# The first four units of a gated linear attention with a bilinear feed-forward behind it, laid out anew

## Chip, cores and metric

One core of a Trainium2 chip. The metric is device time in microseconds (us) of one execution. The engines are TensorE (PE, matmul; PEld is its weight load), VectorE (DVE), ScalarE (ACT), GpSimd (POOL) and SyncE (SP, which issues most DMAs). Each works through its own instructions in program order and waits only where one of them needs something that another engine or a DMA has not delivered yet.

## What is computed

```python
f = 1.0 / (1.0 + np.exp(-f_logit))                 # B, H, S, D = 4, 8, 768, 48
for t in range(S):
    state = f[:, :, t, :, None] * state + np.einsum('bhd,bhe->bhde', k[:, :, t], v[:, :, t])
    y[:, :, t] = np.einsum('bhd,bhde->bhe', q[:, :, t], state)
x = y.transpose(0, 2, 1, 3).reshape(B * S, H * D)  # 3072 x 384
out = (x @ w_a) * (x @ w_b) @ w_out                # d_ff 1536; weights arrive as float64
```

## The kernel before

**Units.** The attention is cut into 16 units: one batch, half of the sequence (384 tokens) and four heads each. Units 0 and 1 make block 0 of x (384 tokens x 384 channels), units 2 and 3 the second half of the same batch, block 1, and so on. There are three sets of input tiles (q, k, f, v); unit u uses set u % 3. Units 0 to 3 are written out by hand; the later ones and the feed-forward are laid by a planner with costs and due times, which the change doesn't touch.

**A unit's front** (`front_parts`, four parts): ACT takes two sigmoids of f (L301, L304), POOL an affine (L307); DVE scans the running products of f forward (`scan_f`, L311, and a small check L314); DVE restarts and scans the inverse in six pieces (L319, L324); DVE multiplies q by the products and k by the inverses (`times`, L328).

**A unit's core**: `scores` (PE, q against k, L374), `mask` (DVE, L397), `turn` (PE transposes of k, L409) and `turned` (ACT copies them to kT, L411), `gains` (PE, kT against v, L433), `carry` (DVE adds them up to states, L454, L456) and `hand_on` (DVE, L465, for the second half of the sequence), `within` (PE, masked scores against v, L476), `across` (PE, states against q, L497), `out_of_bank` (copies of y out of PSUM, L522, on ACT, for units 0 and 1 partly on DVE) and `stored` (DMAs of y into xT, the transposed x of a block, L545).

**Feed-forward.** `up(blk, ft)` multiplies one 128-column tile of w_b and one of w_a by xT (three contraction tiles each, `emit`, L589), `product` copies the first to SBUF (ACT, L609) and multiplies (DVE, L611). Up to unit 3, five pairs of block 0 are spread over the hand-written order; then comes (1, 0), (1, 1), (0, 5) and so on.

**Weights.** Twenty pieces are loaded as 64-bit words (L249) and converted: `begin` does two steps of ACT work (L58, L59, then L62, L63) with a minimum on POOL (L60), `end` the last on DVE (L68, L70). Pieces 0 and 1 hold tile 0 of w_b and w_a, pieces 2 and 3 tiles 1 and 2, pieces 4 and 5 tiles 3 and 4, pieces 6 and 7 tiles 5 and 6. Pieces 4 and 5 are loaded into a part of `groups` that is free by then, the others into four places in turn.

**PSUM.** ps_x and ps_y have two banks each, ps_f0 to ps_f3 one each; `idle` lists those of ps_f that are free. Before, `scores` and `turn` took banks of ps_f when called with `spare`, else ps_x; gains always go to ps_x; y of unit 1 to ps_f, of the others to ps_y. The SBUF copy of y, `y_sb`, comes from a pool with one buffer, so unit 1's copies wait until unit 0's y is stored.

**Order.** A call in the hand-written part puts its instructions at the end of each engine's queue. So the order of the calls is the order on every engine, SP's too.

Of the kernel before, what the change touches and what calls it, by code (L numbers as in the profile page):

```python
# [26 lines left out]
R = 64  # L27
# [106 lines left out]
def by_quotients(ctx, tc, q, k, f_logit, v, moe_w_a, moe_w_b, moe_w_out, out, ident, weights, bad):  # L134
# [156 lines left out]
    def front_parts(u):  # L291

        t = sets[u % NSET]
        x = halves(t["f"])
        F = halves(products_of_f[u])
        inv = invs[u % 2 if u < 2 * NQ else 0]
        none = zero.broadcast_to((128, BLK))
        got = {}

        def sigmoid():  # L300
            nc.scalar.activation(F, x, AF.Sigmoid)  # L301

        def opposite():
            nc.scalar.activation(inv, x, AF.Sigmoid, bias=less, scale=-1.0, accum_out=tails[:, u:u + 1])  # L304

        def affine():
            nc.gpsimd.tensor_scalar(inv, inv, EXP_K, 1.0, ALU.mult, ALU.add)  # L307

        def scan_f(n):
            c = slice(n * BLK, n * BLK + BLK)  # L310
            nc.vector.tensor_tensor_scan(F[:, c], F[:, c], none, math.exp(MIDDLE), ALU.mult, ALU.add)  # L311

        def hold():
            nc.vector.tensor_tensor(held[:, u], products_of_f[u][:, :, BLK - 1], least, ALU.is_ge)  # L314

        def restart():
            got["start"] = sb2.tile([128, 2, NC - 1], FP32, tag="start", name="start")
            by_chunk = products_of_f[u].rearrange("p n (c m) -> p n c m", m=C)
            nc.vector.reciprocal(got["start"], by_chunk[:, :, 0:NC - 1, C - 1])  # L319

        def scan_inv(n, c):
            w = slice(n * BLK + c * C, n * BLK + c * C + C)
            first = got["start"][:, n, c - 1:c] if c else math.exp(-MIDDLE)
            nc.vector.tensor_tensor_scan(inv[:, w], inv[:, w], none[:, 0:C], first, ALU.mult, ALU.add)  # L324

        def times(nm, by):
            live.setdefault(u, {})
            nc.vector.tensor_tensor(halves(t[nm]), halves(t[nm]), by, ALU.mult)  # L328

        first = ((ACT, 930, opposite), (ACT, 750, sigmoid))  # L330
        return (
            [*(first[::-1] if u in FIRST else first), (POOL, 830, affine)],
            [(DVE, 870, scan_f, 0), (DVE, 870, scan_f, 1), (DVE, 80, hold)],
            [(DVE, 90, restart), *((DVE, 385, scan_inv, n, c) for n in range(2) for c in range(NC))],
            [(DVE, 880, times, "q", F), (DVE, 880, times, "k", inv)],
        )
# [9 lines left out]
    y_banks = [ps_y[:, p] for p in range(2)]  # L346
# [12 lines left out]
    def pair(spare=False):  # L359

        return [ps_f[idle.pop(0)] if spare else ps_x[:, i] for i in range(2)]

# [3 lines left out]
    def scores(u, spare=False):  # L366
        t = sets[u % NSET]
        qf, kf = halves(t["q"]), halves(t["k"])
        ps = pair(spare)
        for n, c, o in each():  # L370
            for h in range(2):
                for p in range(2):
                    r = slice(R * h, R * h + D)
                    nc.tensor.matmul(  # L374
                        ps[h][SUB * p:SUB * p + SUB, o:o + SUB],
                        lhsT=kf[r, tokens(n, c, p)],
                        rhs=qf[r, tokens(n, c, p)],
                        start=True,
                        stop=True,
                    )  # L380
        live[u]["scores"] = ps
        if spare is not None:
            mask(u, spare)

    def mask(u, spare=False):

        ps = live[u].pop("scores")
        at = sb1.tile([128, 2, BLK], FP32, tag="at", name="at")
        both = [(at[:, h], ps[h][:, 0:BLK]) for h in range(2)] if spare else [(at, ps_x[:, :, 0:BLK])]
        for to, x in both:  # L390
            lead = x.shape[1:-1]
            letters = "h"[:len(lead)]
            to, x = (y.rearrange(f"s {letters} (o t) -> s {letters} o t", t=SUB) for y in (to, x))
            tri = causal.unsqueeze(1)
            for _ in lead:
                tri = tri.unsqueeze(1)
            nc.vector.tensor_tensor(to, x, tri.broadcast_to((128, *lead, 2 * NC, SUB)), ALU.mult)  # L397
        live[u]["at"] = at
        give_back(ps)

    def turn(u, spare=False):

        kf = halves(sets[u % NSET]["k"])
        kT = sb1.tile([128, 2, NC, 128], FP32, tag="kT", name="kT")
        ps = pair(spare)
        for n in range(2):
# [3 lines left out]
            if spare:  # L410
                nc.scalar.copy(kT[:, n].rearrange("s c x -> s (c x)"), ps[n][:, 0:BLK])  # L411
        live[u]["kT"] = kT
        if not spare and spare is not None:
            turned(u)
        give_back(ps)

    def turned(u):

        nc.scalar.copy(live[u]["kT"].rearrange("s n c x -> s n (c x)"), ps_x[:, :, 0:BLK])

    def gains(u, all=True):
# [3 lines left out]
        last = half == NH - 1  # L425
        for n in range(2):
            for c in range(NC):
                for p in range(2):
                    if last and c == NC - 1 and p == 1:
                        continue  # L430
                    for h in range(2):
                        r = slice(SUB * p, SUB * p + SUB)
                        nc.tensor.matmul(  # L433
                            ps_x[R * h:R * h + D, p, (n * NC + c) * D:(n * NC + c) * D + D],
# [4 lines left out]
                        )  # L439
        st = sb3.tile([128, NJ, 2, D], FP32, tag="st", name="st")  # L440
        before = live[u - NQ]["st"][NJ] if half else None
        live[u]["st"] = [before] + [st[:, j] for j in range(NJ - 1 if last else NJ)]
        if all:
            for j in range(len(live[u]["st"]) - 1):
                carry(u, j)
            hand_on(u)

    def carry(u, j):
# [3 lines left out]
        new = ps_x[:, p, 0:2 * NC * D].rearrange("r (n c d) -> r n c d", n=2, c=NC)[:, :, c]  # L452
# [14 lines left out]
    def within(u, spare=False):  # L467

        t, at = sets[u % NSET], live[u]["at"]
        ps = live[u]["y"] = pair(True) if spare else y_banks  # L470
# [14 lines left out]
    def across(u, all=True):  # L485
# [4 lines left out]
        for n, c, o in reversed(list(each())) if half else each():  # L490
            for p in range(2):
# [13 lines left out]
        if all:  # L505
            for part in range(len(banks_of_y(u))):
                out_of_bank(u, part)
            stored(u)

    def banks_of_y(u):  # L510

        ps = live[u]["y"]
        whole = [(0, 0, 0, 128)] if ps[0] is y_banks[0] else [(0, 0, 0, D), (0, R, R, D)]
        return (*whole, (1, R, 0, D), (1, 0, R, D))

    def out_of_bank(u, part):

        if not part:
            live[u]["y_sb"] = sb1.tile([128, 2 * NC, 2, SUB], FP32, tag="y", name="y")
        p, e, r, rows = banks_of_y(u)[part]  # L520
# [10 lines left out]
    def stores_of(u):  # L531
# [4 lines left out]
        def begin():  # L536
            give_back(live[u].pop("y"))
# [4 lines left out]
        def store(n, h, kt, p, row, w):  # L542
            y = live[u]["y_sb"].rearrange("r (n c) p m -> r n (c p m)", n=2)
            queue = nc.scalar if u < NQ and (n + h) % 2 else nc.sync
# [323 lines left out]
    def core_parts(s):  # L868
# [3 lines left out]
        if u < 2 * NQ:  # L872
            yield PE, 1000, 0, scores, s, None
# [4 lines left out]
        if s < NU:  # L878
            yield DVE, 880, 0, mask, s
            yield PE, 850, 0, turn, s, None  # L880
            yield ACT, 700, 0, turned, s
        if u < 2 * NQ:
            yield PE, 1000, 0, gains, s, False
        elif s < NU:
            yield PE, 1550, 0, gains_and_across, u
        else:
            yield PE, 1000, 0, across, u, False
# [13 lines left out]
    def within_and_scores(u):  # L901
        within(u)
        scores(u + 1, None)

    def gains_and_across(u):
        gains(u + 1, False)
        across(u, False)
# [26 lines left out]
    with tc.manual_schedule():  # L934
# [9 lines left out]
        fronts = [front(u) for u in range(2 * NQ + 1)]  # L944


        load_unit(0, "f")
        load_unit(1, "f")
        next(fronts[0])
        load_unit(1, "q")  # L950
        load_unit(0, "q")
        load_unit(1, "k")
        load_weights()
        load_unit(0, "k")
        load_weights()
        patterns()
        next(fronts[0])
        load_weights()
        next(fronts[0])
        load_unit(1, "v")  # L960
        next(fronts[1])
        next(fronts[1])
        next(fronts[0])
        load_unit(0, "v")
        next(fronts[1])
        begin(3)
        load_unit(2, "k")
        load_unit(2, "f")
        scores(0)
        load_unit(2, "v")  # L970
        next(fronts[1])
        turn(0, True)
        within(0)
        gains(0)
        load_unit(NSET, "f")
        load_weights()
        next(fronts[2])
        turn(1, True)
        across(0)
        load_weights()  # L980
        scores(1, True)
        end(2)
        within(1, True)
        load_unit(2, "q")
        gains(1)
        across(1)
        load_weights()
        next(fronts[2])
        next(fronts[3])
        end(3)  # L990
        next(fronts[2])


        up(0, 0)
        next(fronts[2])
        load_unit(NSET, "q")
        begin(4.5)
        load_weights()
        product()
        load_unit(NSET, "v")  # L1000
        end(4)
        scores(2, True)
        up(0, 1)
        next(fronts[3])
        load_unit(NSET + 1, "q")
        end(5)
        load_unit(NSET, "k")
        end(6)
        within(2)
        load_unit(NSET + 1, "f")  # L1010
        load_unit(NSET + 1, "k")
        turn(2, True)
        load_weights()
        gains(2)
        load_unit(NSET + 1, "v")
        next(fronts[3])
        next(fronts[3])
        product()
        begin(7)
        up(0, 2)  # L1020
        product()
        across(2)
        up(0, 3)
        begin(8)
        scores(3)
        turn(3, True)
        within(3)
        gains(3)
        across(3)
        up(0, 4)  # L1030
        end(7)
        product()
        product()
# [537 lines left out]
```

## Time and profile before

| | us |
|---|---|
| median of 3 runs | 609.38 (608.93 to 611.03) |
| the profiled execution | 609.35 |
| its span, first to last instruction | 607.6 |
| PE busy | 572.1 (94%) |
| DVE busy | 408.7 (67%) |
| ACT busy | 268.8 (44%) |
| first L589 matmul | 32.25 |
| xT of block 0 complete for it | 41.35 |
| xT of block 1 complete | 74.76 |

The profile is that of one execution. Its time is 1.75 us above its span. An fp32 matmul shows as two records. "PEclk" is the granted clock of PE as a share of full speed; times in the timelines count from the first instruction. The busy share of PE from 75 to 135 us is 100%.

### The profile page before, as it was taken

How to read it: one execution, taken by the hardware profiler on the slowest of the kernel's cores; microseconds unless marked ns; L12 is line 12 of the kernel's file. 1: busy time of each engine (PE TensorE's matmuls, PEld its weight loads, DVE VectorE, ACT ScalarE, POOL GpSimd, SP SyncE). 2: the span in 40 equal slices, each digit the busy share in tenths (PEclk: the TensorE clock that was granted, in tenths of full speed). 3: DMA queues.
4: the chain of work that ended last, by engine and by line, in shares of the span. 5: the costliest groups of instructions: out<-in, count | busy, mean ns of one | idle time of the engine just before them, and what ended most of it. 6: DMA issues, size and time to landing. Idle time of an engine off the chain costs nothing.

```text
span 607.6 us, 13865 instructions
## 1 busy us (share of the span) xinstructions
PE 572.1 (94%) x5778; PEld 512.0 (84%) x5778; DVE 408.7 (67%) x762; ACT 268.8 (44%) x508; POOL 74.9 (12%) x69
## 2 busy tenths in 40 slices
PE   0769899999999999999999999999999999999995
PEld 0635555556899999999989999999999999999995
DVE  6778434579979769867895768746775265846741
ACT  5667498962331454326532354326331245134300
POOL 5333164544200000000000000000000000000000
PEclk9959999999999999999999999999999999999999
DMA  8887686139954143025002420022001100000000
GB/s 212 218 253 230 146 258 207 53 63 163 171 127 110 44 98 83 4 82 141 2 2 72 108 70 1 2 76 70 1 3 47 46 0 1 1 28 0 1 29 31
DMA packets 33336, 49.42 MB, mean 81 GB/s; under 512 B 3952, under 2 KB 25072, under 8 KB 33264
## 3 DMA queue, kind: packets, MB, share of 16 engines
q1 hardware_dynamic: 29984, 42.38, 25.3%
q0 software_dynamic: 2992, 5.77, 5.6%
q8 instruction: 47, 0.77, 0.5%
q10 hardware_dynamic: 288, 0.30, 0.2%
q14 instruction: 25, 0.20, 0.1%
HBM read 33.23 MB, written 4.72 MB: 62 GB/s over the span
## 4 chain that ended last, share of the span: by engine, by line
PE 83%; DVE 5%; DMA 4%; ACT 2%; issue 2%; SPq 1%; ACTq 0%; DVEq 0%
PE ps_f L711 34%; PE ps_f L804 27%; PE ps_f L589 14%; DMA xT<-y 2%; PE ps_y L497 2%; PE ps_x L433 2%; PE ps_y L476 2%; PE ps_x L374 2%; DVE groups L703 1%; DMA q_in<-in_q_dram 1%; DVE sums L703 1%; DMA raw<-in_moe_w_a_dram 1%; PE ps_x L409 1%; DVE inv L324 1%; SPq L208 1%
## 5 line engine op out<-in xcount | busy, mean ns | idle before, releaser
L589 PE MATMUL ps_f<-xT,w_ba 128*128 128x384 f32 x288 | 99.6, 504 | 6.4 <-DVE w_ba L70 4.7
L589 PEld LDWEIGHTS ps_f<-xT,w_ba 128*128 128x128 f32 x288 | 55.1, 195 | 46.4 <-DVE w_ba L70 6.6
L1219 ACT COPY sums<-ps_f 128x384 f32<-128x384 f32 x120 | 57.4, 480 | 75.5 <-PE ps_f L711 67.9
L1219 ACT COPY groups<-ps_f 128x384 f32<-128x384 f32 x120 | 57.7, 481 | 63.1 <-PE ps_f L711 41.1
L711 PE MATMUL ps_f<-xT,w_ba 128*128 128x192 f32 x384 | 78.4, 327 | 0.0
L711 PEld LDWEIGHTS ps_f<-xT,w_ba 128*128 128x128 f32 x384 | 64.8, 190 | 0.2
L711 PE MATMUL ps_f<-groups,w_ba 128*128 128x192 f32 x288 | 55.7, 328 | 0.0
L711 PE MATMUL ps_f<-x_sums,raw 128*128 128x192 f32 x288 | 54.0, 331 | 1.2 <-DVE groups L703 0.9
L804 PE MATMUL ps_f<-w_out,sums 128*128 128x192 f32 x288 | 52.2, 329 | 0.1
L804 PE MATMUL ps_f<-w_out,groups 128*128 128x192 f32 x288 | 51.7, 328 | 0.0
L711 PEld LDWEIGHTS ps_f<-x_sums,raw 128*128 128x128 f32 x288 | 46.9, 190 | 4.2 <-DVE groups L703 2.1
L804 PE MATMUL ps_f<-spare,sums 128*128 128x192 f32 x288 | 49.0, 326 | 0.0
L711 PEld LDWEIGHTS ps_f<-groups,w_ba 128*128 128x128 f32 x288 | 47.8, 190 | 0.7 <-ACT groups L1219 0.6
L804 PEld LDWEIGHTS ps_f<-w_out,sums 128*128 128x128 f32 x288 | 47.1, 190 | 1.1 <-DVE groups L611 0.4
L804 PEld LDWEIGHTS ps_f<-w_out,groups 128*128 128x128 f32 x288 | 47.1, 190 | 0.7
L804 PEld LDWEIGHTS ps_f<-spare,sums 128*128 128x128 f32 x288 | 47.1, 190 | 0.1
L60 POOL TENSOR_SCALAR sums<-sums 128x768 f32<-128x768 f32 (+1 forms) x20 | 40.2, 2008 | 51.3 <-ACT sums L58 49.5
L307 POOL TENSOR_SCALAR inv<-inv 128x768 f32<-128x768 f32 x14 | 12.4, 883 | 265.4 <-ACT inv L304 265.3
L703 DVE TENSOR_TENSOR sums<-sums,groups 128x768 f32<-128x768 f32 x36 | 34.7, 964 | 14.2 <-ACT groups L1219 13.7
L703 DVE TENSOR_TENSOR sums<-ps_f,sums 128x384 f32<-128x384 f32 x60 | 32.9, 552 | 16.6 <-PE ps_f L711 15.0
L711 PE MATMUL ps_f<-x_sums,w_ba 128*128 128x192 f32 x192 | 39.3, 327 | 0.3 <-DVE sums L703 0.3
L711 PE MATMUL ps_f<-xT,raw 128*128 128x192 f32 x192 | 39.5, 328 | 0.0
(123 smaller groups left out, 855.4 us busy)
## 6 DMA issues: line engine op xcount, KB each, us to landing
raw<-w_ba POOLq DMA_DIRECT2D x11, 512.0 KB, 8.2
q_in<-in_q_dram SPq DMA_DIRECT2D x32, 144.0 KB, 4.1
k_in<-in_k_dram SPq DMA_DIRECT2D x32, 144.0 KB, 3.5
v_in<-in_v_dram SPq DMA_DIRECT2D x16, 288.0 KB, 4.8
raw<-in_moe_w_out_dram SPq DMA_DIRECT2D x6, 768.0 KB, 4.2
out_dram<-o SPq DMA_DIRECT2D x24, 192.0 KB, 1.9
f_in<-in_f_logit_dram SPq DMA_DIRECT2D x28, 144.0 KB, 3.0
xT<-y SPq DMA_DIRECT2D x46, 72.0 KB, 2.2
```

Of the source, the lines that this page charges most:

```text
L60: nc.gpsimd.tensor_scalar(h, h, HI_MAX, None, ALU.min)
L208: nc.sync.dma_start(out=to, in_=src)
L307: nc.gpsimd.tensor_scalar(inv, inv, EXP_K, 1.0, ALU.mult, ALU.add)
L374: nc.tensor.matmul(ps[h][SUB * p:SUB * p + SUB, o:o + SUB], lhsT=kf[r, tokens(n, c, p)], rhs=qf[r, tokens(n, c, p)], start=True, stop=True,)
L433: nc.tensor.matmul(ps_x[R * h:R * h + D, p, (n * NC + c) * D:(n * NC + c) * D + D], lhsT=kT[r, n, c, R * h:R * h + D], rhs=t["v"][r, n, c, ...
L476: nc.tensor.matmul(ps[p][e:e + D, o:o + SUB], lhsT=t["v"][r, n, c, h * D:h * D + D], rhs=at[r, h, o:o + SUB], start=o == 0, stop=True, ski ...
L497: nc.tensor.matmul(ps[p][e:e + D, o:o + SUB], lhsT=st[j][r, n], rhs=qf[r, tokens(n, c, p)], start=False, stop=True, skip_group_check=True,)
L589: nc.tensor.matmul(ps[nm][:, 0:BLK], lhsT=w[:, kt, ft * 128:ft * 128 + 128], rhs=xT[blk][:, kt], start=kt == 0, stop=kt == NKT - 1,)
L703: nc.vector.tensor_tensor(to, x, y, op)
L711: nc.tensor.matmul(ps[:, g], lhsT=sums_of_w[name][:, g, 128 * j:128 * j + 128], rhs=sums_of_x[blk][name], start=start and g == 0, stop=Tru ...
L804: nc.tensor.matmul(to, lhsT=x[:, i // 2, i % 2], rhs=w[:, NI * (i % 2) + i // 2], start=start and i == 0, stop=i == HFT - 1, skip_group_ch ...
L1219: do(*args)
```

## The change

It reorders the hand-written calls for units 0 to 3 and the transfers between them, and gives each unit fixed PSUM banks.

- **Transfers.** f of units 0 and 1 first, as before; then for each of the two units k, q, one weight piece and v; f of unit 2, pieces 2 and 3. Everything else of unit 2, and of unit 3, and pieces 4 to 7, is issued after the stores of unit 1. All stores of unit 0, and the first half of unit 1's, are issued by SP; the second half of unit 1's by ACT.
- **Place for y.** Unit 1's y is copied to a part of `groups` that nothing else uses at that time.
- **PSUM.** `home(u)` holds scores and y: ps_x for units 0 and 2, ps_y for 1 and 3. `turn` and `gains` use two banks of ps_f (units 0, 1) or `away(u)`: ps_y for unit 2, ps_x for unit 3.
- **Order.** Unit 0's products of k and q, its transposes and scores come ahead of unit 1's scans. k is multiplied before q in every unit. Unit 1's gains are split so that its last chunk follows `within(1)`. Pieces 4 and 5 are begun after the transposes and scores of unit 2. `up(0, 2)` stands before `within(2)`, `up(0, 4)` before `within(3)`; nothing stands between `across(3)` and the first pair of block 1.

```diff
-            [(DVE, 880, times, "q", F), (DVE, 880, times, "k", inv)],
+            [(DVE, 880, times, "k", inv), (DVE, 880, times, "q", F)],
...
+    def home(u):
+        return ps_y if u in (1, 3) else ps_x
+    def away(u):
+        return ps_y if u == 2 else ps_x
...
+            if u == NQ - 1:
+                live[u]["y_sb"] = groups[:, 2 * NTG - 1, PIECE:].rearrange("r (o p m) -> r o p m", p=2, m=SUB)
+            else:
+                live[u]["y_sb"] = sb1.tile([128, 2 * NC, 2, SUB], FP32, tag="y", name="y")
...
-            queue = nc.scalar if u < NQ and (n + h) % 2 else nc.sync
+            queue = nc.scalar if u == NQ - 1 and n else nc.sync
...
+        for u in FIRST:
+            load_unit(u, "f")
+        for u in FIRST:
+            next(fronts[u])
+        patterns()
+        for u in FIRST:
+            load_unit(u, "k")
+            load_unit(u, "q")
+            load_weights()
+            load_unit(u, "v")
+        load_unit(2, "f")
+        load_weights()
+        for _ in range(3):
+            next(fronts[0])
+        begin(1)
+        turn(0)
+        turned(0)
+        scores(0)
+        begin(2)
+        gains(0)
+        for _ in range(3):
+            next(fronts[1])
+        turn(1)
+        turned(1)
+        mask(0)
+        scores(1)
+        next(fronts[2])
+        begin(2.5)
+        carried(0, range(4))
+        within(0)
+        gains(1, range(NC - 1))
+        mask(1)
+        carried(1, range(1))
+        carried(0, range(4, NJ))
+        within(1)
+        gains(1, range(NC - 1, NC))
+        across(0)
+        load_weights()
+        carried(1, range(1, NJ))
+        y_of(0)
+        begin(3)
+        across(1)
+        y_of(1)
+        end(2)
+        load_unit(2, "k")
+        load_unit(2, "q")
+        load_weights()
+        load_unit(2, "v")
+        load_unit(3, "f")
+        load_weights()
+        load_unit(3, "k")
+        load_unit(3, "q")
+        load_unit(3, "v")
+        up(0, 0)
+        begin(4)
+        next(fronts[2])
+        end(3)
+        next(fronts[2])
+        product()
+        end(4)
+        next(fronts[2])
+        load_unit(4, "f")
+        up(0, 1)
+        next(fronts[3])
+        turn(2)
+        turned(2)
+        scores(2)
+        mask(2)
+        product()
+        begin(5)
+        next(fronts[3])
+        up(0, 2)
+        within(2)
+        gains(2)
+        carried(2)
+        begin(6)
+        product()
+        across(2)
+        end(5)
+        y_of(2)
+        load_weights()
+        end(6)
+        next(fronts[3])
+        next(fronts[3])
+        up(0, 3)
+        product()
+        begin(7)
+        turn(3)
+        turned(3)
+        scores(3)
+        mask(3)
+        up(0, 4)
+        within(3)
+        gains(3)
+        carried(3)
+        product()
+        end(7)
+        across(3)
+        y_of(3)
+        load_unit(4, "k")
+        load_unit(4, "q")
+        load_unit(4, "v")
+        load_weights()
+        begin(8)
         end(8)
```

## Prediction

> **What bounds it now.** Read the 40 slices first: where TensorE (PE) is not yet full and where its clock is not.
>
> ```profile
> PE   0769899999999999999999999999999999999995
> ...
> PEclk9959999999999999999999999999999999999999
> ```
>
> One slice is 15.2 us. PE is full from the sixth slice on, so nothing the change touches matters unless it moves the moment from which PE is dense. The chain of work in order of time gives that moment:
>
> ```profile
> 23.70 1.13 PE ps_y L497 x34
> ...
> 28.25 5.49 DMA xT<-y
> ...
> 36.29 4.93 DMA xT<-y
> 41.35 5.10 PE ps_f L589 x8
> ...
> 58.98 4.10 PE ps_f L589 x12
> ...
> 72.38 2.24 DMA xT<-y
> 74.76 66.19 PE ps_f L589 x204
> ```
>
> Block 0's activations land at 41.35, block 1's at 74.76; from there 66 us run without a hole. So I forecast the start of the third contraction tile of the first product of block 1 (74.76 before), and carry its shift to the end, adding clock losses. The PE timeline shows the holes between (columns: start, length, line, tiles, count, idle time before):
>
> ```profile
> 32.25 1.65 PE L589 MATMUL ps_f<-xT,w_ba 128*128 128x384 f32 x2
> 38.55 1.65 PE L589 MATMUL ps_f<-xT,w_ba 128*128 128x384 f32 x2 [4.66 <-DVE w_ba L70]
> 41.35 0.98 PE L589 MATMUL ps_f<-xT,w_ba 128*128 128x384 f32 x1 [1.15 <-DMA xT<-y]
> ...
> 54.03 4.14 PE L589 MATMUL ps_f<-xT,w_ba 128*128 128x384 f32 x12
> ...
> 67.69 1.16 PE L497 MATMUL ps_y<-q_in,st 48*48 48x64 f32 x48 [1.21 <-DVE st L456]
> 68.78 5.43 PE L589 MATMUL ps_f<-xT,w_ba 128*128 128x384 f32 x16
> 74.76 17.50 PE L589 MATMUL ps_f<-xT,w_ba 128*128 128x384 f32 x53 [0.55 <-DMA xT<-y]
> ```
>
> A matmul is two records, a pair of products (b and a) twelve. After unit 3's last matmuls (67.69 to 68.85) the 16 records at 68.78, up(0, 4) and a bit, cover the whole road of y to xT: only 0.55 us is lost. The granted clock by stretches (PE busy first, PEclk after POOL):
>
> ```profile
> 25.48:28.89 3.41, 1.76 (x102) 1.50 (x100) 3.06 (x7) 0.22 (x1) 0.00 (x0) 1.00 0.53 174
> 28.89:35.72 6.83, 4.64 (x88) 2.98 (x76) 4.45 (x13) 0.95 (x2) 0.00 (x0) 0.50 0.68 179
> ...
> 42.55:45.96 3.41, 3.41 (x6) 1.66 (x5) 1.02 (x2) 3.35 (x5) 2.25 (x1) 0.50 1.06 297
> 45.96:53.00 7.04, 7.04 (x116) 4.33 (x114) 6.20 (x10) 4.38 (x6) 2.90 (x2) 1.00 1.00 294
> ```
>
> With PE about half idle in 3.41 us the clock falls to 0.50 and comes back only after 3.41 us full. At half clock eight records take 5.10 us (0.64 each), at full twelve take 4.07 (0.34).
>
> **Opening: up to xT of block 0.** VectorE (DVE) sets it. Unit 0's scans stay at 6.22 to 11.47. Before, unit 1's forward scans stood next; now unit 0's two products follow, 2 x 0.87 = 1.7, to 13.2. Their data: transfers land in issue order, 0.7 us per 144 KB, and k and q of unit 0 now stand right behind f, so near 8.3 and 9.7. Unit 1: scans 2.1 (11.47 to 13.61) and 2.4 (15.35 to 17.77), products 1.7: 19.5. Unit 0's transposes, scores and gains fit beside this (PE rows 1.5, 1.6, 1.2; early rows, as here). Then mask(0) 0.9 and four carries 1.1 on DVE; on PE transposes and scores of unit 1 end at 21.8, within(0) 23.3, two thirds of gains(1) 24.1, within(1) 25.6, the rest 26.0; the remaining carries and hand-on of unit 1 1.8: 27.8; across(1) 1.2: 29.0; its copies 1.1: 30.2. The two conversions' last parts (0.87 each) end at 32, under the stores. SyncE (SP): all five stores of unit 0 are now its own (0.62 each, 28.5 to 31.6), then three of unit 1: 33.5, with 0.6 and 1.9 to landing the last lands by 34.9. If the small matmuls run at their later rows (0.86 for scores, not 1.6), 1 to 2 us less. I take **34.4 in place of 41.35: 7.0 earlier**. The cause of 41.35 was the wait of unit 1's copies for unit 0's stores (33.86, DVE idle 1.97 before) and stores queued behind 768 KB of weights; both go. The last eight records at half clock, 5.1: up(0, 0) ends at 39.5 (46.45 before).
>
> **Middle: the conversions of pieces 4 and 5.** Before, ScalarE (ACT) began them ahead of unit 2's chain:
>
> ```profile
> 42.34 0.88 ACT L58 ACTIVATE sums<-groups 128x768 f32<-128x768 f32 x1
> ...
> 46.37 0.90 ACT L58 ACTIVATE sums<-groups 128x768 f32<-128x768 f32 x1
> ```
>
> A piece costs 3.7 on ACT (42.34 to 46.37 with one copy). Now they stand behind turned(2). In order: up(0, 1) needs piece 3, finished on DVE only after product (0, 0): 39.5 + 0.6 + 1.5 = 41.6, and its second half takes 2.05: 43.7; transposes of unit 2 0.88: 44.6. From there ACT: kT copy 0.9, copy of (0, 1) 0.4, two pieces 7.3, copy of (0, 2) 0.45; DVE: product 0.55, last part of piece 4 1.5, latencies 0.25: **up(0, 3) can start at 55.9**. Meanwhile PE has scores 0.86, up(0, 2) 4.07, within 0.82, gains 0.72, then waits 1.5 for the carries (covered by a product pair before), across 0.82: done at 53.4. Idle 1.5 + 2.5.
>
> Loads hold no longer than that: SP reaches k of unit 2 at 33.5; 3.0 to the first landing, then by queue rows (0.7 per 144 KB, 2.05 per 768 KB) f of unit 3 lands at 42.9. ACT's two sigmoids of it (1.7) end at 44.6, just beside the transposes; each us later would be a us on everything behind. SP has nothing to issue from about 13 to 28, since unit 2's loads stand behind the stores in its queue. GpSimd (POOL) is no bound: both affines now come ahead of the patterns (0.85 each, due at 11.5 and 15.3), and clearing f for unit 3 comes after piece 2's minimum, near 27, before SP is there.
>
> **Tail.** DVE after piece 4: piece 5's last part 1.5, inverse scans of unit 3 2.2 to 3.4 (rows at 56.34 and 38.41; 2.8), k product 0.87: 61.1, while up(0, 3) ends at 60.0. Transposes and scores 1.75, up(0, 4) 4.07: within(3) starts at 67.0. Before, within(3) at 65.07 led to 74.76 in 9.7, all of it chain: gains, carries, across, three copies, five stores, landing. The length stays, so **76.7, 1.9 late**. But the cover, up(0, 4), is gone: it now stands before within(3). After across only the first two tiles of block 1 (1.4) are left in 5.9 us: idle about 4.4.
>
> **Clock.** The row says what such a hole does: 1.65 us idle in 3.41 gave half clock, and it came back 3.41 full us later. At least 3.41 us at half is 1.7 lost, up to 3.4 with two stretches; I take 2.2. The hole of 4 us in the middle slows up(0, 3) by 0 to 1.7, of which 1.1 is hidden by the wait for unit 3's k; I take 0.5. The Trainium skill, "TensorE: Matmul & The Clock Gate", section "Why this matters for your kernels", warns of gaps over about 3 us between bursts and speaks against this order. By it the tail's hole costs a window and the middle's two shorter holes nothing, 0.5 less than my sum; the row at 25.48 shows a fall after less.
>
> **Sum.** -7.0 opening, +4.0 middle holes, +1.2 wait for unit 3's k, about +3.7 of tail (4.4 idle less 0.55 and the carry difference) give +1.9 on the end; + 2.2 + 0.5 for the clock = **+4.6**. The profiled execution took 609.35 with a span of 607.6; the median of the runs is 609.38, so the same base: 614.0. After 74.76 the program order is as before, and ACT's next piece follows the first copy of block 1 in both, so nothing there gives time back.
>
> **Rivals.**
> 1. *The opening gains more and all of it passes* (ends faster). If unit 1's stores land at 32.4 and the clock is already full at 0.34 a record, up(0, 0) ends at 35.1, 4.4 earlier. DVE, ACT and the conversions hang on it; f of unit 3 moves with the stores' end, only 2. Between 2 and 4.4 early, the tail stands at 74.7 to 72.3; without a clock loss 609.3 to 606.9. It decides where up(0, 0) ends before 36. For it: 1.00 was granted from 25.48 in the old trace; against: the idle stretch before xT is still some 4 us. Chance 0.12.
> 2. *The holes cost no clock and the opening is 1 better*: 609.35 + 0.9 = 610.2; for it 67:75 busy 6.76 of 8 at full clock. Chance 0.12.
> 3. *Loads come late*: everything for units 2 and 3 and pieces 4 to 7 is asked for after 33.5. If f of unit 3 lands 2 to 4 later, ACT's in-order queue puts it on kT, both pieces and up(0, 3): 616 to 618. For it: 768 KB issued among others at 39.61 landed at 49.87. Chance 0.16, with the rest (0.60) on the forecast, 611.5 to 616.
> That unit 1's own place does nothing is excluded: its copies go to a part of groups that no earlier store reads.
>
> **Numbers.** About 0.3% (1.8 us) is what a measurement here can tell from no change. Faster 0.12, same 0.12, slower 0.76. The range takes in rival 1's middle and rival 3's end: 607.5 to 618.
>
> **What would show it.** Right: first dense product 33 to 36; up(0, 3) near 56 after idle on a w_ba write; 4 to 5 us idle before block 1's third tile, at 76 to 78; PEclk under 1 after it. Wrong: up(0, 3) with no wait (then the middle is mis-sized), or block 1 before 74.

## The result and the profile after

| | before | after |
|---|---|---|
| median of 6 runs of each on one chip | 608.53 (607.45 to 611.03) | 614.99 (613.03 to 615.86) |
| the profiled execution, its span | 609.35, 607.6 | 615.86, 614.1 |
| third tile of the first product of block 0 | 41.35 | 35.1 |
| up(0, 3) starts | 58.98 | 58.09 |
| `within(3)` starts | 65.07 | 70.50 |
| third tile of the first product of block 1 | 74.76 | 80.21 |
| last matmul starts | 600.75 | 607.51 |

The ratio is 1.0096, with a 95% interval of 1.0071 to 1.0122: slower by 6.5 us. The profiled execution after is the longest of its six, at a mean granted clock of 0.974 where the other five show 0.979 to 0.982, so the clock it lost is an upper end. The opening won 6.2 us, and at the start of up(0, 3) 0.9 of them was left. The 40 slices of the changed kernel:

```profile
PE   1586889999999999999999999999999999999995
...
PEclk9878979999999999999999999999999999999998
```

PE stays at 9 tenths from the seventh slice on, not from the sixth, and the clock, which only the third slice had lacked before, is now short in four of the first six. The PE timeline of the changed kernel tells where (start, length, line, tiles, count, idle before):

```profile
33.70 8.44 PE L586 MATMUL ps_f<-xT,w_ba 128*128 128x384 f32 x16 [0.75 <-DMA xT<-groups]
...
52.73 1.16 PE L501 MATMUL ps_x<-q_in,st 48*48 48x64 f32 x48 [1.22 <-DVE st L460]
58.09 6.91 PE L586 MATMUL ps_f<-xT,w_ba 128*128 128x384 f32 x12 [4.20 <-DVE w_ba L70]
...
66.43 4.14 PE L586 MATMUL ps_f<-xT,w_ba 128*128 128x384 f32 x12
...
78.03 1.62 PE L586 MATMUL ps_f<-xT,w_ba 128*128 128x384 f32 x2 [2.81 <-DMA xT<-y]
80.21 6.09 PE L586 MATMUL ps_f<-xT,w_ba 128*128 128x384 f32 x12 [0.56 <-DMA xT<-y]
```

The row at 33.70 begins with the two records of the second tile; the third tile follows them at 35.1. Two holes answer to the two that were forecast: 4.20 before up(0, 3), and after unit 3's last matmuls 2.81 and 0.56 around the first two tiles of block 1, where before 0.55 was all. And up(0, 3), twelve records, takes 6.91, while up(0, 4) at 66.43 takes 4.14 for the same work. The clock tells why. Stretches of the changed kernel (length, PE, PEld, DVE, ACT and POOL busy, PEclk, DMA share, GB/s):

```profile
53.49:56.91 3.42, 0.40 (x28) 0.25 (x16) 0.99 (x2) 3.35 (x7) 1.52 (x1) 1.00 0.18 52
...
56.91:63.73 6.82, 5.64 (x9) 3.19 (x10) 6.47 (x13) 1.77 (x4) 0.05 (x1) 0.50 0.52 134
...
77.39:84.21 6.82, 5.62 (x9) 2.71 (x10) 1.52 (x2) 4.49 (x7) 2.62 (x2) 0.50 0.78 170
```

Each hole is followed by 6.82 us at half clock, in which up(0, 3) and the first products of block 1 run. Last, what up(0, 3) waited for is piece 4, finished on DVE only behind product (0, 2), whose copy stands behind both pieces on ACT. ACT's timeline:

```profile
45.48 0.94 ACT L304 ACTIVATE spare<-f_in,less 128x768 f32<-128x768 f32 x1 [8.37 <-DMA f_in<-in_f_logit_dram]
...
47.29 0.78 ACT L415 COPY kT<-ps_y 128x768 f32<-128x768 f32 x1
...
55.44 0.45 ACT L606 COPY x_sums<-ps_f 128x384 f32<-128x384 f32 x1
```

ACT stood idle for 8.37 us for f of unit 3. The transposes of unit 2 were done at 45.2, but the kT copy had to follow f's sigmoids; from it to the copy of product (0, 2) at 55.44 there is no pause.

The loss adds up so, from before to after: up(0, 3) starts 0.9 earlier; it takes 2.8 longer (6.91 for 4.10); up(0, 4) now stands ahead of `within(3)` and moves it by some 3.6 more, in all 5.4; from `within(3)` to block 1's third tile it is 9.7 in both; and the next 26 records, the first of them at half clock, take 10.4 in place of 8.5: 7.4 late. Of these 0.7 come back up to the last matmul.

### The profile page after: what moved, and what is told of

Read it like the earlier page. It is cut to its first block, busy times and chain, and to the rows that moved or that the text cites. A ratio compares the mean times of both kernels' runs of the same rounds, so it can differ in the third digit from the quotient of the medians.

```text
span 614.1 us, 13863 instructions
## 1 busy us (share of the span) xinstructions
PE 574.0 (93%) x5778; PEld 512.5 (83%) x5778; DVE 411.4 (67%) x760; ACT 268.0 (44%) x505; POOL 76.2 (12%) x69
## 4 chain that ended last, share of the span: by engine, by line
PE 82%; DVE 8%; issue 3%; DMA 3%; ACT 2%; POOL 1%; SPq 1%; DVEq 0%; ACTq 0%; POOLq 0%
PE ps_f L708 34%; PE ps_f L801 26%; PE ps_f L586 13%; PE ps_y L501 2%; PE ps_y L480 2%; DVE sums L700 1%; PE ps_x L430 1%; DVE inv L324 1%; PE ps_x L382 1%; PE ps_x L406 1%; DMA groups<-in_moe_w_b_dram 1%; DVE groups L700 1%; POOL sums L60 1%; DMA q_in<-in_q_dram 1%; DVE groups L311 1%
## 5 line engine op out<-in xcount | busy, mean ns | idle before, releaser
L586 PE MATMUL ps_f<-xT,w_ba 128*128 128x384 f32 x288 | 105.1, 525 | 12.6 <-DMA xT<-y 7.4
L586 PEld LDWEIGHTS ps_f<-xT,w_ba 128*128 128x128 f32 x288 | 58.0, 205 | 55.6 <-issue 12.2
L1241 ACT COPY sums<-ps_f 128x384 f32<-128x384 f32 x120 | 57.3, 480 | 76.1 <-PE ps_f L708 59.9
L708 PEld LDWEIGHTS ps_f<-xT,w_ba 128*128 128x128 f32 x384 | 64.8, 190 | 0.2
```

The costliest lines, as they stand in the source:

```text
L586: nc.tensor.matmul(ps[nm][:, 0:BLK], lhsT=w[:, kt, ft * 128:ft * 128 + 128], rhs=xT[blk][:, kt], start=kt == 0, stop=kt == NKT - 1,)
L708: nc.tensor.matmul(ps[:, g], lhsT=sums_of_w[name][:, g, 128 * j:128 * j + 128], rhs=sums_of_x[blk][name], start=start and g == 0, stop=Tru ...
L1241: do(*args)
```

## The experiments

All are timed beside the kernel before on the same chip; "useless" matmuls are ones whose product nothing reads.

| run | median us | ratio to before (95%) |
|---|---|---|
| after | 614.99 | 1.0096 (1.0071 to 1.0122) |
| after, cover put back (e1) | 612.19 | 1.0060 (1.0039 to 1.0080) |
| after, loads earlier (e2) | 615.02 | 1.0111 (1.0094 to 1.0128) |
| after, holes filled (e3) | 612.47 | 1.0062 (1.0045 to 1.0079) |
| before, cover taken away (e4) | 615.19 | 1.0100 (1.0082 to 1.0118) |
| before, own place for y (e5) | 607.84 | 0.9978 (0.9968 to 0.9987) |
| the same, hole filled (e5w) | 606.14 | 0.9948 (0.9935 to 0.9961) |
| after, cover and filling (e6) | 609.31 | 1.0008 (0.9996 to 1.0019) |
| combined version (e7) | 611.57 | 1.0044 (1.0032 to 1.0057) |
| e6 and early loads (e8) | 610.38 | 1.0026 (1.0015 to 1.0038) |
| combined version, mended (e9) | 602.55 | 0.9899 (0.9884 to 0.9915) |
| after, shared place for y (e10) | 617.64 | 1.0146 (1.0127 to 1.0164) |
| e6, piece 4 first (e11) | 607.99 | 0.9990 (0.9979 to 1.0001) |

The theory: the opening's gain is used up in the middle, by the conversions behind unit 2's chain on ACT, and the loss comes from the cover that up(0, 4) gave and from the clock after both holes. The rival: loads that come late set the middle, and the holes cost nothing of themselves.

### The cover: e1 and e4

```diff
 mask(3)
-up(0, 4)
 within(3)
...
-product()
 end(7)
 across(3)
 y_of(3)
+up(0, 4)
+product()
```

> The changed kernel with one pair of products put back: up(0, 4) stands again behind across(3) and the stores of unit 3. Theory (the uncovered tail costs, and its clock loss with it): within(3) starts 4.1 us earlier (66.4 instead of 70.5), and from it 9.7 us to the third tile of block 1, now 76.1 instead of 80.21; the idle before it falls from 3.4 us to under 1 and the half clock from 77.39 to 84.21 (about 1.9 lost) is gone: 5 to 6 us less than the changed kernel, near 609.5. Rival (the tail is hidden anyway, since conversions or the planner behind it set the end): within 1.5 us of the changed kernel.

Measured 612.19, 2.8 back (2.2 by the ratios) where the expectation had twice that. The PE timeline of this run:

```profile
70.38 8.97 PE L586 MATMUL ps_f<-xT,w_ba 128*128 128x384 f32 x20
79.86 20.59 PE L586 MATMUL ps_f<-xT,w_ba 128*128 128x384 f32 x63 [0.51 <-DVE w_ba L70]
```

Now 20 records cover the way of y to xT, and the hole is gone. But they take 8.97, not 6.7: with up(0, 4) gone from between mask and `within(3)`, a wait of 1.11 (mask) came up there beside the 1.29 (states) that the changed kernel has too, and the clock stood at 0.50 from 68.13 to 74.95. Block 1's third tile ran at 77.9 within that row, though its data had landed at 76.16, near the 76.1 of the expectation: PE was not yet through with up(0, 4). So the same pair can cover one place or the other, and e1 lost the clock all the same.

The counterpart, the kernel before with its cover taken away:

```diff
 begin(8)
+up(0, 4)
+product()
 scores(3)
 turn(3, True)
 within(3)
 gains(3)
 across(3)
-up(0, 4)
 end(7)
 product()
-product()
 end(8)
```

> The kernel before with one move: up(0, 4) put ahead of unit 3's scores instead of behind its across; one product moves with it. Theory (the cover is worth what it hides): 4.1 us of work no longer lie beside the road of y, and 9.7 us from within(3) now start 4.1 us later; with the clock falling in the new hole of about 4.5 us, 1.7 to 2 more: 5 to 6 us more than before, 613.5 to 615. Rival (other work of the chain is late anyway): under 2 us more.

Measured 615.19. Its PE timeline:

```profile
60.16 8.01 PE L589 MATMUL ps_f<-xT,w_ba 128*128 128x384 f32 x24
...
77.58 1.62 PE L589 MATMUL ps_f<-xT,w_ba 128*128 128x384 f32 x2 [2.84 <-DMA xT<-y]
79.83 20.45 PE L589 MATMUL ps_f<-xT,w_ba 128*128 128x384 f32 x54 [0.64 <-DMA xT<-y]
```

The holes of 2.84 and 0.64 are the changed kernel's (2.81 and 0.56), made by this one move in a kernel with the old opening, the old banks and the old transfers. That the starts agree as well is chance: in this execution (616.84) up(0, 1), which stands ahead of the move, already began 1.25 later than in the kernel before (48.49 for 47.24). From the start of up(0, 3) to block 1's third tile it is 19.7 here (60.16 to 79.83), 15.8 in the kernel before: 3.9 of the loss. Behind the tile 5.66 us more are at half clock, some 2.8 lost by estimate. One move costs 6 to 7 us there (615.19 against 608.49 beside it, 1% by the ratio), hole and clock (0.50 from 75.25 to 85.49) together.

### The clock: e3 and e6

`idle_work` lays as many useless matmuls of 128 x 384 as its second argument says.

```diff
 across(2)
+idle_work(ps_y, 6)
...
 across(3)
+idle_work(ps_x, 5)
```

> The changed kernel with eleven extra matmuls whose results nothing uses: six behind across(2), five behind across(3), each 128x384 from weights and block 0's activations. They fill the two long idle stretches of PE without bringing anything forward. Theory (the holes lower the granted clock, and that costs beyond the holes): no half clock from 56.9 to 63.7 nor from 77.4 to 84.2; up(0, 3) takes 4.1 instead of 6.9 us and block 1's first products 8.2 instead of 10: 2 to 3.5 us less than the changed kernel, 611.5 to 613. Rival (the clock costs nothing, or the extra matmuls delay the real ones): the same or up to 3 us more.

Measured 612.47, as the clock theory had it. The timeline of PE in this run:

```profile
57.81 4.11 PE L586 MATMUL ps_f<-xT,w_ba 128*128 128x384 f32 x12
62.45 0.85 PE L406 MATMUL ps_x<-ident,k_in 128*128 128x128 f32 x6 [0.53 <-ACT spare L59]
63.90 0.93 PE L382 MATMUL ps_y<-q_in,k_in 48*64 48x64 f32 x48 [0.60 <-DVE q_in L328]
...
78.53 21.74 PE L586 MATMUL ps_f<-xT,w_ba 128*128 128x384 f32 x66 [1.13 <-DMA xT<-y]
```

up(0, 3) begins 0.3 earlier than in the changed kernel and takes 4.11 in place of 6.91; the granted clock is 1.00 from 37.39 to the last matmul. Not all of that is won: PE now waits 0.53 and 0.60 for DVE's products of unit 3's k (done at 62.35) and q. Nothing but the filling was changed, so 2.5 us of the loss (2.1 by the ratios) are the clock.

Both together, e6: e1's order, and 10 useless matmuls in three places.

```diff
 across(2)
+idle_work(ps_y, 6)
...
 mask(3)
+idle_work(ps_f[idle[0]].unsqueeze(1), 2)
...
 end(7)
+idle_work(ps_f[idle[0]].unsqueeze(1), 2)
 across(3)
```

> The changed kernel with up(0, 4) behind across(3) as in the kernel before, and 10 matmuls that nothing uses in the holes that this leaves (6 behind across(2), 2 behind scores(3), 2 behind the states of unit 3). If the clock is what is left of the loss there, up(0, 3) takes 4.1 instead of 6.2 and block 1's first products run at full clock: 609.5 to 610.5 against 612.2 without the filling. If the rest of the loss is the late start of up(0, 3) alone (ACT and f of unit 3), 611.5 to 612.5.

Measured 609.31, ratio 1.0008: level with the kernel before. Cover and clock together are thus the whole loss against the kernel before. It also says where the opening went: with both repaired, 6.2 us of earlier xT give nothing. Its PE timeline:

```profile
57.52 4.03 PE L586 MATMUL ps_f<-xT,w_ba 128*128 128x384 f32 x12
...
75.53 24.69 PE L586 MATMUL ps_f<-xT,w_ba 128*128 128x384 f32 x75 [0.52 <-DMA xT<-y]
```

up(0, 3) starts 1.5 ahead of the kernel before (58.98), block 1's third tile 0.8 behind it (74.76): the middle has eaten most of the gain before up(0, 3), and unit 3's chain the rest (18.0 from the one to the other in place of 15.8).

### The loads: e2 and e8

e2 asks for k and q of unit 2, f of unit 3 and v of unit 2 right after piece 3, and no longer behind unit 1's stores (those lines are left out here), while SP otherwise issues nothing until unit 0's stores:

```diff
 across(0)
 load_weights()
+load_unit(2, "k")
+load_unit(2, "q")
+load_unit(3, "f")
+load_unit(2, "v")
```

> The changed kernel with k, q, v of unit 2 and f of unit 3 issued ahead of unit 0's stores, in the 5 us in which the DMA queues stand still (23.3 to 28.5). Theory (late loads put 2.2 us on the middle: ACT waited until 45.38 for f of unit 3): f lands before 31, the kT copy of unit 2 follows its transposes at 45.2 instead of 47.29, pieces 4 and 5 land some 4 us earlier, up(0, 3) starts near 56.0 instead of 58.09 and all behind it 2 us earlier: 612.5 to 613.5. Rival (the loads ahead delay the stores of y): the first product starts 1 to 3 us later and the end is the same or later, 615 to 617.

Measured 615.02, no gain. f landed at 29.8 in place of 45.4, yet the opening was 1.3 later: f's load waited in SP for POOL to clear its tile, and the first store followed 0.36 later than in the changed kernel; before the fifth SP waited 1.2 more, which the profile puts down to the landing of an earlier store. Its PE timeline:

```profile
57.32 5.50 PE L586 MATMUL ps_f<-xT,w_ba 128*128 128x384 f32 x12 [2.24 <-DVE w_ba L70]
...
78.04 22.24 PE L586 MATMUL ps_f<-xT,w_ba 128*128 128x384 f32 x59 [0.56 <-DMA xT<-y]
```

And its stretches around that row (columns as above):

```profile
70.39:73.80 3.41, 2.00 (x50) 1.19 (x50) 2.67 (x7) 1.47 (x4) 0.00 (x0) 1.00 0.00 0
...
77.21:80.63 3.42, 2.86 (x5) 1.51 (x5) 1.20 (x2) 1.11 (x3) 0.00 (x0) 0.50 0.88 214
80.63:84.04 3.41, 3.41 (x7) 1.79 (x6) 0.45 (x1) 3.38 (x5) 2.12 (x1) 0.50 1.09 230
```

Block 1's third tile comes 2.2 earlier than in the changed kernel (80.21). Of this 0.8 is the earlier start of up(0, 3), and 1.4 its length: here half clock ended at 60.14, after one stretch and not two. But in the tail the clock fell one stretch earlier, and came back at 84.04, against 84.21 there: what was won was run at half clock. So e2 tells nothing against late loads; it tells that a gain of 2 us behind such a hole can vanish.

e8 puts the same four lines into e6, where the clock stays up:

> The run with the cover put back and the holes filled (609.31), and with it the early loads (k and q of unit 2, f of unit 3 and v of unit 2 asked for after piece 3, ahead of unit 0's stores). In the filled run ACT still waits 7.29 for f of unit 3 until 44.73, and the clock can no longer eat what is gained. If the late f is what keeps the opening's gain from the end (the prediction's third rival), up(0, 3) starts 1.5 to 2.5 earlier and the time is 607 to 608. If the delay of the opening by those loads (1.3 in the early-load run) and the two conversions on ACT take it back, 609 to 610.

Measured 610.38, and inconclusive by a fault of the experiment, as its PE timeline shows:

```profile
55.26 4.14 PE L945 MATMUL ps_y<-xT,w_ba 128*128 128x384 f32 x12
59.23 4.03 PE L586 MATMUL ps_f<-xT,w_ba 128*128 128x384 f32 x12
```

The useless matmuls (L945) run to 59.4, while DVE had piece 4 done at 57.4: the filling itself held up(0, 3) by some 1.7. ACT's row shows more: its kT copy came at 46.71 (46.54 in e6), since the opening's delay had moved unit 2's transposes by as much as the early f had won.

### The order on ACT: e11

Against e6, and with 2 useless matmuls behind `across(2)` in place of 6:

```diff
+load_weights()          # piece 4
 load_unit(2, "k")
 load_unit(2, "q")
-load_weights()
+load_unit(3, "f")
 load_unit(2, "v")
-load_unit(3, "f")
 load_weights()
...
 up(0, 1)
+begin(5)
 next(fronts[3])
...
 product()
-begin(5)
```

> The run with the cover put back and the holes filled (609.31), with one thing of the middle turned round: piece 4 is asked for first behind unit 1's stores, f of unit 3 ahead of unit 2's v, and piece 4 is begun on ACT ahead of the sigmoids of unit 3 and of unit 2's kT copy, in the 7.29 us in which ACT waits for f of unit 3; 2 useless matmuls behind across(2) in place of 6. If the order of the conversions on ACT is what holds up(0, 3) (the prediction's middle step), it starts near 54.7 in place of 57.5 and the time is 606.3 to 607.5. If the moved transfers make k and q of unit 2 and the kT copy late by as much, or block 1's third tile hangs on unit 3's chain alone: 608.5 to 610.

Measured 607.99, half a us above the expected range, and 0.18% below e6 by the ratios, whose intervals just overlap (1.1 us; 2.0 by the spans, 605.9 and 607.9). ACT converts piece 4 from 37.75 in what had been its idle time, f is there at 42.2, and the kT copy starts at 45.45. On PE:

```profile
55.38 4.03 PE L586 MATMUL ps_f<-xT,w_ba 128*128 128x384 f32 x12
...
73.41 26.78 PE L586 MATMUL ps_f<-xT,w_ba 128*128 128x384 f32 x81 [0.54 <-DMA xT<-y]
```

up(0, 3) starts 2.1 earlier than in e6, and block 1's third tile too: in these two executions what the middle wins reaches the end, with the clock kept. e11 moved transfers as well (f landed 2.5 earlier than in e6), so it doesn't part the order on ACT from the loads. It stops at 55.38, not at 54.7, as DVE finishes piece 4 at 55.06 behind unit 2's carries.

### The opening: e5, e5w and e10

e5 is the kernel before with the own place for unit 1's y and nothing else; e10 takes the same lines out of the changed kernel; e5w is e5 with 8 useless matmuls.

```diff
+            if u == NQ - 1:
+                live[u]["y_sb"] = groups[:, 2 * NTG - 1, PIECE:].rearrange("r (o p m) -> r o p m", p=2, m=SUB)
+            else:
...
         across(1)
+        idle_work(8)
```

> One part of the change alone: the kernel before, with the copy of unit 1's y in its own place, nothing else moved. Theory: the copies no longer wait for unit 0's stores (DVE was idle 1.97 us before them at 33.86), so xT of block 0 comes complete 2 to 3 us earlier (38.5 to 39.5 in place of 41.35), and PE is dense enough behind it to pass it on: 606 to 607.5. Rival one: the stores still stand behind pieces 4 and 5 in SP's queue and the transfers, xT moves by less than 1, time unchanged (608 to 609). Rival two: xT moves, but ACT's and DVE's conversions set up(0, 3), or the clock comes back at the same moment as before (45.96), and the time is unchanged.

> As the run before it (the kernel before with the own place), and 8 matmuls that nothing uses (128 x 384, about 0.7 us each at full clock) behind across(1), in the hole ahead of the first products. Clock theory: the hole's half clock (28.89 to 45.96) ends before xT is complete, the eight records of up(0, 0) take 2.7 instead of 5.1 us, and the time falls by 2 to 4 against the kernel before: 605 to 606.5. Rival: from 42 on ACT's and DVE's conversions set the pace, and what PE wins is waited away before up(0, 1) or up(0, 3): 607.5 to 609.

> The changed kernel with one part undone: unit 1's y goes to the one shared buffer again, so that its copies wait until unit 0's five stores have landed (32.7 in the changed kernel, copies at 28 to 30 there). Then the third tile of the first product comes about 3 later, 37.5 to 38.5, and with SP later free f of unit 3 lands 2 to 3 later. If the opening passes on to the end: 617 to 618.5. If the middle has slack against the opening (ACT and the clock's grid set up(0, 3) alone): 614.5 to 616.

e5 took 607.84, 1.1 less than the kernel before beside it (608.91): xT is complete at 40.05, 1.3 earlier and not the 2 to 3 expected, block 1's third tile comes at 73.81 in place of 74.76, so most of it reaches the end. e5w took 606.14. Its PE timeline:

```profile
33.40 8.21 PE L953 MATMUL ps_f<-k_in,ident 128*128 128x384 f32 x16 [1.27 <-DVE groups L525]
41.45 4.03 PE L592 MATMUL ps_f<-xT,w_ba 128*128 128x384 f32 x12
```

The filling ends 1.4 after e5's xT was complete, so it is too long, yet all of up(0, 0) then runs in 4.03 at full clock, and the next pair begins at 46.27, as in e5 (46.23). The two have the same profile from there to the end, with spans of 606.4 and 606.3, and e5w's profiled execution took 608.08, more than its median. So its 1.7 us against e5 are in the medians, and where they come from stays open.

e10 took 617.64, 2.7 more than the changed kernel (3.0 by the ratios). The copies waited for unit 0's stores, as ACT's row shows:

```profile
33.39 0.48 ACT L516 COPY y<-ps_y 128x384 f32<-128x384 f32 x1 [4.38 <-DMA xT<-y]
```

The first tiles then come at 36.09, the third at 39.0, 3.9 later. By the medians the own place is worth more in the changed kernel than in the kernel before, and part of the opening's gain passes. The way isn't shown: the profiled execution took 615.71, less than e10's median, and in it block 1's third tile comes at 80.44, near the changed kernel's 80.21. There up(0, 3) starts 1.3 later (59.41) but takes 5.80, with one stretch at half clock in place of two.

### Combined versions: e7 and e9

Both keep the new opening and fill the hole ahead of up(0, 0) with 8 useless matmuls. k and q of unit 2 and f of unit 3 are asked for early, piece 4 is begun ahead of `turn(2)` (piece 5, unlike what e7's expectation says, only behind unit 2's kT copy, at 44.41 in e7), pairs are split over the waits for masks and states, and up(0, 4) stands (e9: two thirds of it) behind `across(3)`. The core of e7 against the changed kernel:

```diff
 across(0)
 load_weights()
+load_unit(2, "k")
+load_unit(2, "q")
+load_unit(3, "f")
...
 end(2)
+idle_work(ps_f[2], 8)
+load_weights()
+load_weights()
...
+end(3)
-up(0, 0)
+part_of_up(0, 6)
...
 next(fronts[3])
+begin(5)
 turn(2)
...
+part_of_up(3, 3)
 within(3)
 gains(3)
+part_of_up(3, 3)
 carried(3)
...
 across(3)
 y_of(3)
...
+part_of_up(4, 6)
```

`part_of_up(ft, n)` lays the next n of the six steps of up(0, ft).

> A version to beat both kernels: the changed kernel's opening; k, q of unit 2, f of unit 3 and one weight piece asked for before unit 0's stores; pieces 4 and 5 begun on ACT ahead of unit 2's transposes, and piece 3 ended ahead of up(0, 0); each of up(0, 2) and up(0, 3) split into halves that cover the waits for mask and states; up(0, 4) behind across(3); 8 matmuls that nothing uses ahead of up(0, 0), for the clock. If the middle was late by the order on ACT and by f, up(0, 3) begins before 55, block 1's third tile comes at 71 to 74, and the time is 606.5 to 608.5, then held by pieces 6 and 7. If the conversions on ACT and DVE are the bound themselves, the early start is waited away and it is 609 to 611.

Measured 611.57, a miss. Block 1's third tile came near 67, but then ACT waited for a weight piece, in its timeline:

```profile
80.57 0.90 ACT L58 ACTIVATE sums<-raw 128x768 f32<-128x768 f32 x1 [5.03 <-DMA raw<-in_moe_w_a_dram]
```

PE waited behind it, 2.96 before 84.58 and 1.24 before 86.74. That piece was asked for only behind unit 3's stores, at 72.31, and landed at 80.49. It was neither of the two expected reasons: the consumers had been moved ahead, and their load had not. Besides, the clock stood at 0.50 from 52.32 to 59.14, after a wait of 1.60 for unit 2's states and through one of 1.58. The core of e9 against e7:

```diff
 end(4)
+load_weights()          # pieces 8 and 9
+load_weights()
...
 across(2)
+product()
+end(6)
 y_of(2)
-load_weights()
...
-product()
-end(6)
```

> The combined version again, with what its trace showed mended: pieces 8 and 9 are asked for as soon as piece 4 is ended and not behind unit 2's and unit 3's stores (ACT waited 5.03 for one there, PE 2.96 and 1.24), piece 5 is ended and product (0, 2) taken ahead of unit 3's inverse scans, up(0, 4) covers the wait for unit 3's states and its copies. If those waits are all that kept it at 611.6, about 4.3 comes back in the tail and 2 to 5 in the middle: 603 to 606, below the best version so far (606.14). If ACT's conversions or the clock take the place of the waits: 607 to 610.

Measured 602.55, 1% (0.84 to 1.16%) below the kernel before, and the best here. The clock row of its page:

```profile
PEclk9999999999999999999999999999999999999999
```

Two rows of its PE timeline:

```profile
50.72 4.14 PE L586 MATMUL ps_f<-xT,w_ba 128*128 128x384 f32 x12
...
68.73 31.52 PE L586 MATMUL ps_f<-xT,w_ba 128*128 128x384 f32 x97 [1.30 <-DMA xT<-y]
```

up(0, 3) starts 8.3 and block 1's third tile 6.0 ahead of the kernel before, and the clock never falls before the last matmul. Many things were turned at once, so no part of this is put down to a single edit.

## Why the prediction was right, and where its sizes were not

It gave 614.0 and the runs gave 614.99; its mechanism (a late up(0, 3), the lost cover, the clock behind the holes) stands, as e1, e3, e4 and e6 show. Its shift was too small, +4.6 against 6.5, which the base (609.4 against 608.5 in the runs beside the changed kernel) hid in part.

- **Opening, 34.4 forecast, 35.1 measured.** The stores of unit 1 landed at 34.13, and up(0, 0) ended at 40.2 (39.5).
- **up(0, 3) at 55.9, measured 58.09.** The order on ACT was right; the kT copy was forecast for 44.6 and came at 47.29. The step that failed is "Loads hold no longer than that": f of unit 3 landed at 45.38, not 42.9. Piece 4, ahead of it, landed 5.2 after unit 2's q (37.78 to 43.00), where a queue row of 2.05 had been used. This is the third rival's condition, at its lower end (f 2 to 4 later). e11 shows that 2 us of the start are to be had from this order.
- **Holes, 1.5 + 2.5, measured 1.22 + 4.20**, the second longer by the same late f.
- **The wait for unit 3's k, 1.2, did not show**: with up(0, 3) slow, k was ready. In e3, with up(0, 3) fast, PE waited 0.53 for k and 0.60 for q. So it lay hidden under the slow clock, as the forecast had said of 1.1.
- **`within(3)` to block 1's third tile: 9.7 forecast, 9.71 measured.** So the error of 3.5 in that tile (76.7 forecast) all arose before `within(3)`.
- **Clock.** In the tail 2.2 forecast and 2.0 measured. In the middle the forecast had 0.5 on top of the wait of 1.2, in all 1.7, and the profiled execution 2.8: two stretches at half clock where the forecast had allowed for one. The row quoted at 25.48 was the right guide, not the size taken from it. In e1, with the same order up to there, up(0, 3) took 6.16, so 2.8 is not every execution's. That the clock "comes back only after 3.41 us full" holds for the row quoted, but not in e2 and e10 (below).
- **Nothing gives time back later**: 0.7 of 7.4 came back. The reason given was wrong: in the changed kernel ACT's next piece began at 75.92, ahead of the first copy of block 1 (81.86).
- **Signs.** Block 1's third tile came at 80.21, outside the 76 to 78 forecast, with 3.4 us idle around its first two tiles, not 4 to 5.
- **Rivals.** The first (up(0, 0) ending before 36) did not come: PE ran at half clock until 39.84. The second (no clock cost) is refuted by e3. The third's condition came true, but not its price of 616 to 618. That 614.0 came so near is partly luck: f's lateness (2.2) and the middle's clock (1.1 more than allowed) were offset in part by the 0.7 that came back and by the base, 0.9 lower.

## What to carry to other kernels

A pair of matmuls that covers a chain's end is worth the hole it fills and the clock behind it: moving one call cost 6 to 7 us of 609 here, and an opening 6 us earlier did not win that back. Follow an early start to the next engine that must convert, copy or load for it, and see whether that engine's queue and its loads have moved along; where they have not, the gain ends there. When a hole can't be closed, ask in which stretch it lies before counting a small gain behind it.

## What the runs showed of the hardware

- **The clock's fall.** The clock changed on a grid of 3.41 us. It fell after stretches with PE busy for 0.40 and 1.24 us (the changed kernel), 1.76 (the kernel before) and 2.00 (e2), and stayed after 2.12 and 2.19 (the changed kernel at 70.56 and 50.08). Busy time alone doesn't set it: it also stayed after 1.88 in e9 (from 66.09) and after 2.00 in e7 (from 79.62). What else counts isn't shown.
- **The clock's return.** It came back after full stretches, but also after 2.82 of 3.41 in e2 (from 56.73) and 2.89 in e10 (from 79.92), while 3.04 in the kernel before (from 28.89) and 2.86 in e2 (from 77.21) did not suffice. Where PE was idle again meanwhile, half clock lasted: 10.2 us in e2 (from 73.80) and 17.1 in the kernel before (from 28.89), each after a stretch with less than 1.7 us idle.
- **The page's rule.** The Trainium skill, "TensorE: Matmul & The Clock Gate", section "Why this matters for your kernels", warns of gaps over about 3 us. The runs show a fall after less: the clock of the kernel before fell at 28.89, with a single gap of 1.51 us and 1.65 us idle in all in the stretch before, and the measurement decides.
- **The transfers.** In the changed kernel their share was 0.02 and 0.10 in the two stretches from 22.78 to 29.60, and 1.00 from 36.43 to 39.84. Piece 5 took 12.0 us from issue to landing there. An issue's place among others, not its size alone, set its time: a load of 144 KB took 2.9 us from issue to landing at 32.91 and 10.9 at 39.03.
